# Batch 0 and 1 attention scores with tokens on the partitions, 21 instructions moved to GpSimd, and a rewritten start order

## The chip, the cores and the metric

The kernel runs on one core of a Trainium2 chip. The metric is the device time of one execution in microseconds; the median of several runs counts. A core has five engines that run side by side, each through its own list of instructions in order: TensorE (PE, with its weight loads shown apart as PEld), VectorE (DVE), ScalarE (ACT), GpSimd (POOL) and SyncE (SP), which here issues the loads and stores.

## The reference

The kernel computes an attention over 32 memory slots per head, and feeds the result to a two-layer network. There are 8 batches, 8 heads, 576 tokens, head size 64; the network goes from 512 to 2048 channels and back.

```python
a = softmax(phi, over the 32 slots)                 # phi: b h s m
k_m = einsum("bhsm,bhsd->bhmd", a, k)               # slots of K
v_m = einsum("bhsm,bhsd->bhmd", a, v)               # slots of V
attn = softmax(q @ k_m.T / 8, over the 32 slots)    # b h s m
x = (attn @ v_m) with heads as channels             # 4608 x 512
h = x @ w_in
out = where(h > 0, h, exp(min(h, 0)) - 1) @ w_out
```

## The kernel before

All matrix products are kept at full precision by splitting each operand into a high part and a remainder (HI, LO) and adding three products (PASSES). V's slots are multiplied into w_in ahead of time (`vw`), so that per batch the network's first layer is one product of `vw` with the attention weights `A`.

The work is cut into iterations `it`. One iteration is a batch, a half of its tokens (288, `HALF`) and one block of 128 of the 2048 channels: `hidden` (six PE products into a PSUM bank), `elu_exp` (two ACT instructions), `elu_max` (DVE), `rest_copy` (POOL, the last 32 tokens of the half), `elu_high` (ACT) and `elu_low` (DVE, the remainder), and `project` (six PE products). Iterations 0 to 2 are batch 0's first half, 3 to 5 its second, 6 and 7 its fourth block in both halves; iteration 8 is the first of batch 1.

Before batch 0's first `hidden` stands its attention: `load_phi`, `phi_max`, `phi_exp`, `e_transpose` and `e_copy` turn phi's exponentials; `slots` multiplies them with K or V; `slots_copy`, `slots_transpose` and `kv_copy` put the slots into the tile `kvm`. `scores` multiplies `kvm` with a unit of queries, slots on the partitions. `turn` (DVE, 32x32 block transposes, two instructions per unit) puts tokens on the partitions; `softmax_max`, `softmax_shift`, `softmax_exp`, `softmax_sum` and `softmax_divide` do the softmax; `turn_back` (DVE) transposes back; `probs_high` (ACT) and `probs_low` (DVE) write the two parts of `A`. Batch 0 has three units (160, 128 and 288 tokens), batch 1 two of 288, later batches three of 192.

The weights arrive as 64-bit numbers in 32 tiles k of 128x512 (`load_raw`); even and odd groups of them are w_in (into `win`) and w_out (into `wout`). Each goes through `dec_mag` and `dec_low` (ACT), `dec_sign`, `dec_top` and `dec_add` (DVE; `dec_add` is an addition of 32-bit integers, L410), and for w_out also `dec_high` (ACT) and `dec_rest` (DVE, L424).

Each engine takes its instructions in the order in which the steps are written. For the start, until iteration 64, this order is a list written out by hand, FIRST; an entry such as `vw.0.0.128.256` is a step's name and its arguments. After it a plan sorts the steps by due times; it is the same in both kernels. Loads go through SP's queue in the order of FIRST. Tiles come out of pools with a fixed number of buffers, and an instruction waits for a free one: `gf` has 5, the hidden products' PSUM tile `psh` 2, the raw weight tiles 4 per tag. `warm_up.n` multiplies the identity with itself n times; its result is not used.

## Time and profile before

| | before |
|---|---|
| median of 3 runs (lowest, highest) | 720.07 us (719.92, 722.39) |
| the profiled execution: time, span | 720.75 us, 719.0 us |
| PE busy | 698.5 us (97%) |
| DVE busy | 463.2 us (64%) |
| ACT busy | 459.5 us (64%) |
| POOL busy | 43.4 us (6%) |
| mean granted TensorE clock | 0.985 |
| DMA | 64.45 MB, mean 90 GB/s |

The span runs from the first to the last instruction. An engine's share of the span is an average over stages with different limits, so the stages are read one by one, from windows. Two more things help with the rows below. A matmul of 32-bit floats (f32) is two instructions in the profile, a transpose is one, and a matmul in the format fp32r is one. And a row "x6" merges six instructions that follow each other, with the time that the six took together; in brackets stands how long the engine sat idle before it, and what ended that. In a shape such as "64*32 64x288" the stationary block is 64x32 and the moving one 64x288.

### The profile page before, as it was taken

How to read it: one execution, taken by the hardware profiler on the slowest of the kernel's cores; microseconds unless marked ns; L12 is line 12 of the kernel's file. 1: busy time of each engine (PE TensorE's matmuls, PEld its weight loads, DVE VectorE, ACT ScalarE, POOL GpSimd, SP SyncE). 2: the span in 40 equal slices, each digit the busy share in tenths (PEclk: the TensorE clock that was granted, in tenths of full speed). 3: DMA queues.
4: the chain of work that ended last, by engine and by line, in shares of the span. 5: the costliest groups of instructions: out<-in, count | busy, mean ns of one | idle time of the engine just before them, and what ended most of it. 6: DMA issues, size and time to landing. Idle time of an engine off the chain costs nothing.

```text
span 719.0 us, 13493 instructions
## 1 busy us (share of the span) xinstructions
PE 698.5 (97%) x5050; PEld 575.7 (80%) x5050; DVE 463.2 (64%) x1221; ACT 459.5 (64%) x1102; POOL 43.4 (6%) x88
## 2 busy tenths in 40 slices
PE   7788999999999999999999999999999999999997
...
GB/s 291 361 258 85 171 31 117 122 133 59 137 30 81 205 31 1 96 144 92 1 1 110 145 91 1 13 97 193 31 1 37 90 189 30 2 30 1 30 1 44
DMA packets 24977, 64.45 MB, mean 90 GB/s; under 512 B 3408, under 2 KB 7632, under 8 KB 24912
## 3 DMA queue, kind: packets, MB, share of 16 engines
...
q10 hardware_dynamic: 96, 0.13, 0.1%
HBM read 54.13 MB, written 9.44 MB: 88 GB/s over the span
## 4 chain that ended last, share of the span: by engine, by line
PE 88%; DVE 6%; DMA 3%; ACT 2%; issue 0%; SPq 0%; DVEq 0%; ACTq 0%
PE pso L749 54%; PE psh L688 27%; PE psb L530 3%; DMA kvt<-kv 3%; PE psb L481 2%; PE pso L530 2%; DVE gf L712 1%; DVE top L403 1%; ACT gf L704 0%; DVE wout L424 0%; DVE top L410 0%; ACT gf L703 0%; DVE win L403 0%; DVE win L410 0%; DVE gp L741 0%
## 5 line engine op out<-in xcount | busy, mean ns | idle before, releaser
L749 PE MATMUL pso<-wout,gp 128*128 128x512 f32 x1728 | 444.8, 396 | 0.8 <-ACT orest L812 0.5
L749 PEld LDWEIGHTS pso<-wout,gp 128*128 128x128 f32 x1728 | 310.2, 188 | 66.8 <-issue 2.9
L688 PEld LDWEIGHTS psh<-A,vw 128*128 128x128 f32 x1536 | 229.4, 189 | 40.1 <-issue 10.5
L688 PE MATMUL psh<-A,vw 128*128 128x288 f32 x1536 | 247.7, 298 | 6.7 <-DVE vw L650 3.1
L715 DVE SCALAR_TENSOR_TENSOR gf<-gf,psh 128x256 f32<-128x256 f32 x192 | 80.7, 420 | 144.8 <-ACT gf L704 144.7
L703 ACT ACTIVATE gf<-psh 128x288 f32<-128x288 f32 x256 | 104.7, 409 | 103.2 <-PE psh L688 101.5
L735 ACT CAST gp<-gf 128x256 fp32r<-128x256 f32 x256 | 103.1, 404 | 80.7 <-DVE gf L715 65.7
L741 DVE TENSOR_TENSOR gp<-gf,gp 128x256 fp32r<-128x256 f32 x256 | 108.8, 427 | 52.5 <-ACT gp L735 51.6
L704 ACT ACTIVATE gf<-gf 128x288 f32<-128x288 f32 x256 | 113.9, 445 | 8.1
L291 POOL TENSOR_TENSOR e<-e,nmb 128x512 f32<-128x512 f32 (+1 forms) x18 | 20.7, 1178 | 364.0 <-DMA nmb<-nmd 275.7
L712 DVE SCALAR_TENSOR_TENSOR gf<-gf,psh 128x288 f32<-128x288 f32 x64 | 28.6, 449 | 12.3 <-ACT gf L704 11.5
L723 DVE SCALAR_TENSOR_TENSOR rest<-gf,psh 128x32 f32<-128x32 f32 x192 | 34.6, 180 | 0.0
L731 POOL COPY rest<-gf 128x32 f32<-128x32 f32 x64 | 22.1, 360 | 171.6 <-DVE gf L712 171.5
L650 DVE TENSOR_TENSOR vw<-psb,vw 128x512 fp32r<-128x512 f32 (+2 forms) x48 | 26.9, 582 | 2.0 <-ACT vw L644 2.0
L793 ACT CAST gp<-rest 128x256 fp32r<-128x256 f32 x32 | 12.5, 404 | 22.0 <-PE pso L749 22.0
L798 DVE TENSOR_TENSOR gp<-rest,gp 128x256 fp32r<-128x256 f32 x32 | 13.1, 421 | 16.1 <-ACT gp L793 16.1
L644 ACT CAST vw<-psb 128x512 fp32r<-128x512 f32 (+2 forms) x48 | 22.4, 496 | 0.4 <-PE psb L530 0.4
L530 PE MATMUL psb<-win,kvm 64*32 64x512 f32 (+2 forms) x384 | 22.6, 527 | 0.0
L381 ACT ACTIVATE mag<-raw 128x512 uint32<-128x512 uint32 x30 | 19.9, 673 | 3.3 <-DVE win L403 1.6
L377 ACT ACTIVATE mag<-raw 128x512 f32<-128x512 f32 x30 | 19.6, 665 | 0.0
L650 DVE TENSOR_TENSOR vw<-pso,vw 128x512 fp32r<-128x512 f32 (+1 forms) x28 | 17.2, 624 | 0.0
L481 PE MATMUL psb<-kvt,e 128*32 128x128 f32 (+1 forms) x480 | 15.1, 274 | 0.0
...
## 6 DMA issues: line engine op xcount, KB each, us to landing
...
```

The lines of the kernel that those rows point to most:

```text
L481: nc.tensor.matmul(ps[32 * j : 32 * j + 32, a], s["e"][c // 2][:r, c % 2, x : x + M], kv_rows(b, c, i, 2 * j + a), start=(c == 0 and a == ...
L530: nc.tensor.matmul(outs[a][32 * j : 32 * j + 32, :], lhs[r, 32 * j : 32 * j + 32], rhs[r, j], start=True, stop=True, tile_position=(64 * a ...
L650: nc.vector.tensor_tensor(t[:, LO, a, n0:n1], s["ps"]["vw", c, n0][a], t[:, HI, a, n0:n1], ALU.subtract)
L688: nc.tensor.matmul(ps, t[:, x, g, c0 : c0 + P], s["A"][hf][:, y, g, :], start=(n == 0), stop=(n == 5),)
L703: nc.scalar.activation(gf, ps, AF.Relu, scale=-1.0)
L704: nc.scalar.activation(gf, gf, AF.Exp, scale=-1.0)
L712: nc.vector.scalar_tensor_tensor(gf, gf, -1.0, ps, ALU.add, ALU.max)
L715: nc.vector.scalar_tensor_tensor(gf[:, :n], gf[:, :n], -1.0, ps[:, :n], ALU.add, ALU.max)
L723: nc.vector.scalar_tensor_tensor(rest_of(b, j)[:, o : o + REST], gf[:, n:], -1.0, ps[:, n:], ALU.add, ALU.max)
L735: nc.scalar.copy(gp[:, HI], gs[it][:, : NT * P])
L741: eng.tensor_tensor(gp[:, LO], gf[:, : NT * P], gp[:, HI], ALU.subtract)
L749: nc.tensor.matmul(ps, gp[:, y], wout[j][:, x, :], start=(first and n == 0), stop=(last and n == 2),)
```

## The change

Seven things change at once.

1. In batches 0 and 1 a unit is now half of the tokens (288), and `scores` uses `by_token`: the queries are the stationary block (64 channels x 128 tokens) and the 32 slots the moving one, so the result has tokens on the partitions. The last 32 tokens of a half are done with the slots as before, but also with tokens on the partitions.
2. `turn` is gone there. `softmax_max` and `softmax_shift` read the scores from PSUM, each in two instructions of 288 columns.
3. `back`, new, transposes the weights on PE (four transposes a unit); `turn_back` only transposes the last 32 tokens (two small DVE instructions); `probs_high` and `probs_low` work in two pieces, one of them from PSUM.
4. 18 of the 32 `dec_add` and 3 of the 16 `dec_rest` go from DVE to POOL. `slots_copy` of batch 1 goes from DVE to ACT.
5. There are 38 warm-up products instead of 27.
6. The loads are in another order on SP's queue.
7. FIRST is rewritten up to iteration 64. `hidden` keeps its order except for 5 and 2, 13 and 12, 42 and 40, 60 and 59.

The order up to iteration 8, before and after:

```diff
-tables load_phi.0 phi_max.0.0 load_kv0.K0 load_kv0.K1 load_kv0.T load_raw.0 phi_exp.0.0 phi_max.0.1
-phi_exp.0.1 load_half_q.0.0 warm_up.11 slot_scale.0 load_raw.2 load_kv0.V0 e_transpose.0.1
-e_copy.0.1 e_transpose.0.0 e_copy.0.0 slots.0.0.K.y slots.0.1.K e_transpose.0.2 slots.0.2.K
-slots.0.3.K e_copy.0.2 slots.0.4.K slots_copy.0.K slots_transpose.0.K dec_mag.0 load_raw.1
-load_kv0.V1 dec_sign.0 dec_top.0 kv_copy.0.K dec_low.0 load_raw.3 load_kv.1.1 scores.0.0.yz
-scores.0.1 turn.0.0 turn.0.1 softmax_max.0.0 warm_up.2 warm_up.1 warm_up.2 load_half_q.0.1
-load_phi.1 softmax_max.0.1 softmax_shift.0.0 softmax_shift.0.1 softmax_exp.0.0 dec_add.0
-softmax_exp.0.1 warm_up.1 slots.0.0.V.y slots.0.1.V slots.0.2.V slots.0.3.V slots.0.4.V
-softmax_sum.0.0 slots_copy.0.V slots_transpose.0.V softmax_sum.0.1 load_raw.5 softmax_divide.0.0
-dec_mag.1 softmax_divide.0.1 turn_back.0.0 kv_copy.0.V turn_back.0.1 probs_high.0.0 dec_mag.2
-dec_sign.1 dec_top.1 probs_high.0.1 probs_low.0.0 vw.0.0.0.128.yz vw_high.0.0.0.128 dec_low.1
-dec_sign.2 dec_top.2 vw_low.0.0.0.128 probs_low.0.1 dec_low.2 dec_add.1 hidden.0 dec_mag.3 dec_add.2
-dec_sign.3 dec_top.3 dec_high.1 load_kv.1.0 load_raw.6 load_kv.1.2 elu_exp.0 dec_mag.5 dec_rest.1
-dec_low.3 phi_max.1 scores.0.2.yz vw.0.0.128.256 warm_up.3 vw_high.0.0.128.256 load_kv.1.3
-phi_exp.1.0 load_kv.1.4 phi_exp.1.1 elu_max.0 turn.0.2 vw_low.0.0.128.256 hidden.1 e_transpose.1.1
-e_transpose.1.0 warm_up.3 warm_up.4 softmax_max.0.2 softmax_shift.0.2 elu_exp.1 load_raw.4 dec_add.3
-softmax_exp.0.2 elu_max.1 slot_scale.1 load_raw.12 load_raw.7 load_half_q.1.0 rest_copy.0
-e_transpose.1.2.y elu_high.1 dec_high.3 elu_high.0 e_copy.1.0 softmax_sum.0.2 softmax_divide.0.2
-turn_back.0.2 slots.1.0 slots.1.1 dec_mag.4 dec_sign.4 dec_top.4 dec_sign.5 dec_top.5 probs_high.0.2
-e_copy.1.1 slots.1.2 e_copy.1.2 slots.1.3 dec_mag.7 dec_low.5 slots.1.4 probs_low.0.2 dec_low.4
-dec_mag.6 elu_low.0 dec_add.5 hidden.3 project.0 dec_add.4 dec_high.5 elu_exp.3 slots_copy.1
-dec_rest.3 elu_low.1 elu_max.3 dec_rest.5 vw.0.0.256.384.yz dec_sign.6 dec_top.6 project.1
-vw_high.0.0.256.384 rest_copy.3 rest_copy.1 elu_high.3 slots_transpose.1 vw_low.0.0.256.384
-kv_copy.1 dec_low.6 hidden.4 dec_sign.7 dec_top.7 hidden.2 elu_exp.4 dec_add.6 dec_low.7 scores.1.0
-elu_max.4 elu_exp.2 rest_copy.4 hidden.5 elu_high.4 turn.1.0 elu_max.2 elu_low.3 vw.0.0.384.512
-elu_exp.5 softmax_max.1.0 vw_high.0.0.384.512 rest_copy.2 elu_high.2 vw_low.0.0.384.512
-load_half_q.1.1 scores.1.1.yz hidden.6 elu_max.5 elu_low.2 project.2 vw.1.0.0.256 elu_exp.6
-elu_low.4 softmax_shift.1.0 softmax_exp.1.0 load_raw.9 elu_high.5 hidden.7 dec_mag.12
-vw_high.1.0.0.256 elu_exp.7 turn.1.1 softmax_sum.1.0 elu_max.6 dec_add.7 softmax_divide.1.0
-softmax_max.1.1 project.3 project.4 elu_high.6 load_raw.8 dec_high.7 vw_low.1.0.0.256 elu_max.7
-elu_high.7 dec_mag.9 vw.1.0.256.512 vw_high.1.0.256.512 dec_rest.7 turn_back.1.0 elu_low.5
-softmax_shift.1.1 probs_high.1.0 softmax_exp.1.1 probs_low.1.0 hidden.8 hidden.10 load_raw.17
...
+tables load_phi.0 phi_max.0.0 phi_exp.0.0 phi_max.0.1 phi_exp.0.1 slot_scale.0 warm_up.13
+load_kv0.K0 load_kv0.K1 load_kv0.V1 load_kv0.T load_half_q.0.0 load_raw.0 load_kv0.V0
+e_transpose.0.1 e_copy.0.1 e_transpose.0.0 e_copy.0.0 e_transpose.0.2 e_copy.0.2 warm_up.5
+slots.0.0.K.y slots.0.1.K slots.0.2.K slots.0.3.K slots.0.4.K slots_copy.0.K warm_up.2
+slots_transpose.0.K kv_copy.0.K dec_mag.0 dec_sign.0 dec_top.0 dec_low.0 load_raw.1 load_raw.2
+scores.0.0.yz softmax_max.0.0 warm_up.1 softmax_shift.0.0 warm_up.5 load_half_q.0.1 load_raw.3
+dec_add.0 softmax_exp.0.0 warm_up.2 slots.0.0.V.y slots.0.1.V slots.0.2.V slots.0.3.V slots.0.4.V
+warm_up.1 softmax_sum.0.0 load_raw.6 load_phi.1 load_raw.5 dec_mag.1 dec_mag.2 dec_sign.2 dec_sign.1
+softmax_divide.0.0 dec_top.1 warm_up.1 slots_copy.0.V slots_transpose.0.V kv_copy.0.V
+vw.0.0.0.128.yz vw_high.0.0.0.128 back.0.0.x turn_back.0.0 probs_high.0.0 dec_low.1 dec_top.2
+vw_low.0.0.0.128 dec_sign.3 probs_low.0.0 dec_low.2 phi_max.1 dec_add.1 dec_add.2 dec_mag.3
+warm_up.4 hidden.0 elu_exp.0 dec_mag.5 dec_top.3 dec_sign.5 dec_high.1 dec_low.3 scores.0.1.yz
+vw.0.0.128.256 warm_up.3 vw_high.0.0.128.256 phi_exp.1.0 load_raw.4 load_kv.1.3 load_kv.1.4
+load_kv.1.1 phi_exp.1.1 softmax_max.0.1 vw_low.0.0.128.256 softmax_shift.0.1 dec_rest.1 elu_max.0
+hidden.1 e_transpose.1.0 e_transpose.1.1 softmax_exp.0.1 elu_high.0 load_kv.1.0 load_kv.1.2
+softmax_sum.0.1 dec_top.5 load_raw.9 load_half_q.1.1 load_raw.7 load_raw.11 load_half_q.1.0
+e_copy.1.0 elu_exp.1 dec_mag.4 e_copy.1.1 elu_max.1 elu_low.0 dec_sign.4 softmax_divide.0.1
+dec_add.3 dec_high.3 dec_top.4 slot_scale.1 e_transpose.1.2.y warm_up.1 e_copy.1.2 elu_high.1
+dec_mag.6 dec_low.4 slots.1.0 slots.1.1 slots.1.2 slots.1.3 slots.1.4 back.0.1.b turn_back.0.1
+elu_low.1 dec_rest.3 probs_high.0.1 dec_low.5 dec_mag.7 project.0 probs_low.0.1 hidden.3 dec_add.4
+dec_add.5 vw.0.0.256.384.yz dec_sign.6 slots_copy.1 dec_sign.7 elu_exp.3 dec_top.6 project.1
+rest_copy.1 dec_high.5 slots_transpose.1 dec_low.6 vw_high.0.0.256.384 vw_low.0.0.256.384 kv_copy.1
+hidden.4 dec_rest.5 elu_max.3 dec_top.7 scores.1.0 hidden.5 hidden.2 elu_exp.4 dec_low.7 elu_max.4
+dec_add.6 elu_high.3 rest_copy.4 rest_copy.0 softmax_max.1.0 softmax_shift.1.0 elu_exp.2 elu_max.2
+elu_low.3 vw.0.0.384.512 softmax_exp.1.0 vw_high.0.0.384.512 elu_high.4 rest_copy.3 rest_copy.2
+elu_high.2 elu_exp.5 vw_low.0.0.384.512 load_raw.15 load_raw.8 scores.1.1.yz vw.1.0.0.256 hidden.6
+elu_low.2 softmax_max.1.1 elu_low.4 elu_max.5 project.2 elu_exp.6 softmax_shift.1.1 load_raw.17
+load_raw.10 hidden.7 elu_high.5 elu_max.6 project.3 project.4 load_raw.24 load_raw.12 dec_mag.12
+elu_exp.7 vw_high.1.0.0.256 dec_mag.9 elu_high.6 softmax_sum.1.0 dec_add.7 dec_high.7
+softmax_divide.1.0 back.1.0.h turn_back.1.0 elu_low.5 elu_max.7 elu_high.7 probs_high.1.0
+vw.1.0.256.512 vw_low.1.0.0.256 probs_low.1.0 hidden.8 softmax_exp.1.1 hidden.10 load_raw.13
...
```

The code:

```diff
-             "sc0": 2048, "pr0": 2368, "sc1": 2688, "pr1": 2944, "sc2": 3200, "pr2": 0}
-
-    SPARE1 = {"e0": 0, "e1": 512, "e2": 1024, "x0": 1536,
-              "sc0": 2048, "pr0": 2624, "sc1": 3200, "pr1": 0}
+             "sc0": 2048, "sc1": 2624, "pr0": 3200, "pr1": 3264}
...
     def temp(b, name, i, n):
...
-            o = SPARE1[f"{name}{i}"]
+            o = SPARE[f"{name}{i}"]
...
-    mult_on_pool = ()
-    x_on_act = (0,)
+    mult_on_pool = ((0, 2),)
+    x_on_act = (0, 1)
...
-    rest_on_pool = ()
+    rest_on_pool = (1, 5, 28)
...
-    add_on_pool = ()
+    add_on_pool = (0, 2, 3, 6, 8, 9, 11, 12, 14, 17, 19, 21, 22, 24, 26, 28, 30, 31)
...
     def units(b):
...
-        if b == 0:
-            return (0, 160), (160, 288), (288, 576)
-        if b == 1:
-            return (0, 288), (288, 576)
+        if b < NB:
+            return (0, HALF), (HALF, S)
...
     def bank(shape, where):
...
+    def by_token(outs, q, keys):
+
+        for c in range(NT):
+            for j in range(NPAIR):
+                for a in range(2):
+                    r = slice(64 * a, 64 * a + 64)
+                    n = c * P + j * M
+                    nc.tensor.matmul(
+                        outs[a][:, n : n + M],
+                        q[r, j, c * P : (c + 1) * P],
+                        keys[r, 32 * j : 32 * j + 32],
+                        start=True,
+                        stop=True,
+                        tile_position=(64 * a, 0),
+                    )
+        for a in range(2):
+            for j in range(NPAIR):
+                r = slice(64 * a, 64 * a + 64)
+                nc.tensor.matmul(
+                    outs[a][32 * j : 32 * j + 32, NT * P :],
+                    q[r, j, NT * P :],
+                    keys[r, 32 * j : 32 * j + 32],
+                    start=True,
+                    stop=True,
+                    tile_position=(64 * a, 32 * j),
+                )
+
     def scores(b, u, where="bb"):
...
         ps = [bank([P, q.shape[-1]], x) for x in where]
-        by_head(ps, s["kvm"][:, 0], q)
+        if b < NB:
+            by_token(ps, q, s["kvm"][:, 0])
+        else:
+            by_head(ps, s["kvm"][:, 0], q)
...
     def scores_of(b, own, lent):
...
     def softmax_max(b, u):
+        mx = work.tile([P, 2 * HALF // SQ], F32, name="mx")
+        if b < NB:
+            n = HALF // SQ
+            for a, ps in enumerate(st[b]["ps"]["s", u]):
+                nc.vector.tensor_reduce(
+                    mx[:, a * n : (a + 1) * n],
+                    ps.rearrange("p (n m) -> p n m", m=SQ), AX.X, ALU.max,
+                )
+        else:
+            sc = st[b]["sc"][u]
+            mx = mx[:, : sc.shape[1]]
+            nc.vector.tensor_reduce(mx, sc, AX.X, ALU.max)
+        st[b]["mx", u] = mx
+
+    def softmax_shift(b, u):
+        mx = st[b].pop(("mx", u))
+        if b < NB:
+            n = HALF // SQ
+            sc = temp(b, "sc", u, 2 * HALF).rearrange("p (n m) -> p n m", m=SQ)
+            st[b]["sc"][u] = sc
+            for a, ps in enumerate(st[b]["ps"].pop(("s", u))):
+                g = slice(a * n, (a + 1) * n)
+                nc.vector.tensor_tensor(
+                    sc[:, g], ps.rearrange("p (n m) -> p n m", m=SQ),
+                    mx[:, g].unsqueeze(2).to_broadcast([P, n, SQ]), ALU.subtract,
+                )
+            return
         sc = st[b]["sc"][u]
...
-        mx = work.tile([P, 2 * HALF // SQ], F32, name="mx")[:, :n]
-        nc.vector.tensor_reduce(mx, sc, AX.X, ALU.max)
-        st[b]["mx", u] = mx
-
-    def softmax_shift(b, u):
-        sc = st[b]["sc"][u]
-        n = sc.shape[1]
-        mx = st[b].pop(("mx", u))
         eng = nc.gpsimd if (b, u) in shift_on_pool else nc.vector
...
         eng = nc.gpsimd if (b, u) in mult_on_pool else nc.vector
...
+    def back(b, u, where="b"):
+
+        s = st[b]
+        sc = s["sc"][u].rearrange("p n m -> p (n m)")
+        ps = bank([P, 2, NT * P], where)
+        for a in range(2):
+            for c in range(NT):
+                n = a * HALF + c * P
+                nc.tensor.transpose(ps[:, a, c * P : (c + 1) * P], sc[:, n : n + P], ident)
+        s["ps"]["p", u] = ps
+
     def turn_back(b, u):
...
+        if b < NB:
+            pr = temp(b, "pr", u, 2 * REST)
+            for a in range(2):
+                nc.vector.transpose(
+                    pr[:, a * REST : (a + 1) * REST],
+                    sc[:, (a + 1) * HALF // SQ - 1],
+                )
+            s["pr", u] = pr.rearrange("p (g s) -> p g s", g=2)
+            return
...
     def probs_high(b, u):
...
+        if b < NB:
+            A = s["A"][u] = work.tile([P, 2, 2, HALF], F32R, name="A", bufs=4)
+            nc.scalar.copy(A[:, HI, :, : NT * P], s["ps"]["p", u])
+            nc.scalar.copy(A[:, HI, :, NT * P :], s["pr", u])
+            return
         for hf, src, dst in probs_parts(b, u):
...
     def probs_low(b, u):
...
+        if b < NB:
+            A = s["A"][u]
+            n = NT * P
+            for dst, x in ((slice(0, n), s["ps"].pop(("p", u))), (slice(n, HALF), pr)):
+                nc.vector.tensor_tensor(A[:, LO, :, dst], x, A[:, HI, :, dst], ALU.subtract)
+            return
         eng = nc.gpsimd if (b, u) in low_on_pool else nc.vector
         for hf, src, dst in probs_parts(b, u):
...
-            softmax_divide, turn_back, probs_high, probs_low, vw, vw_high, vw_low, hidden,
+            softmax_divide, back, turn_back, probs_high, probs_low, vw, vw_high, vw_low, hidden,
...
```

173 lines of the change are left out of this document (86 added, 87 removed).

## The prediction

> **What bounds the kernel now.** First the page's table of engines and its 40 slices: PE holds 97% of the span, so time can only come out of the few slices where PE is not at 9.
>
> ```profile
> PE 698.5 (97%) x5050; PEld 575.7 (80%) x5050; DVE 463.2 (64%) x1221; ACT 459.5 (64%) x1102; POOL 43.4 (6%) x88
> ...
> PE   7788999999999999999999999999999999999997
> ```
>
> Then the windows between three landmarks read off PE's timeline: the first hidden product of batch 0 (25.91 us), the first of its second half (hidden.3, 40.38) and the first of batch 1 (hidden.8, 60.60).
>
> ```profile
> 0.00:25.91 25.91, 17.57 (x254) 14.24 (x254) 12.20 (x33) 10.46 (x26) 0.70 (x6) 0.71 0.94 327
> 25.91:40.38 14.47, 11.52 (x155) 9.01 (x155) 14.01 (x30) 11.93 (x26) 0.21 (x1) 0.82 1.03 351
> 40.38:60.60 20.22, 16.97 (x171) 12.02 (x167) 19.70 (x45) 15.51 (x40) 1.65 (x4) 1.00 0.57 210
> 60.60:200.00 139.40, 138.89 (x940) 113.60 (x940) 115.13 (x245) 111.27 (x260) 23.32 (x62) 1.00 0.30 100
> ```
>
> The columns are the busy time of PE, PEld, DVE, ACT and POOL, then granted clock, DMA share and GB/s. After 60.60 PE is busy 138.89 of 139.40 us: what DVE loses there cannot show. Before, three regimes follow each other: DMA (share 0.94), then DMA and DVE together (1.03, and 14.01 of 14.47), then DVE alone (19.70 of 20.22, DMA 0.57). The chain of waits agrees: a load until 20.6 us, then DVE up to hidden.8; its last rows here give PE's prices, 0.80 for a hidden and 1.39 for a project step.
>
> ```profile
> 8.47 12.04 DMA kvt<-kv
> ...
> 59.85 0.70 DVE A L630
> 60.60 1.61 PE psh L688 x10
> ...
> 76.18 0.80 PE psh L688 x6
> 76.98 1.39 PE pso L749 x6
> ```
>
> So the change is worth the shift of hidden.8 in time, less the PE work that it leaves behind that point.
>
> **The change, part by part.** *DVE's relief, 25.91 to 60.60.* Prices, from DVE's timeline (start, duration):
>
> ```profile
> 34.70 0.73 DVE L588 TENSOR_REDUCE sm<-spare 128x18 f32<-128x576 f32 x1
> 35.46 0.18 DVE L589 TENSOR_SCALAR sm<-sm 128x18 f32<-128x18 f32 x1
> ...
> 35.98 0.76 DVE L599 TENSOR_TENSOR spare<-spare,rs 128x576 f32<-128x576 f32 x1
> 36.77 0.78 DVE L605 STREAM_TRANSPOSE spare<-spare 128x576 f32<-128x576 f32 x1
> ...
> 38.58 0.42 DVE L398 TENSOR_SCALAR top<-raw 128x512 uint32<-128x512 uint32 x1
> ...
> 39.64 0.75 DVE L630 TENSOR_TENSOR A<-spare,A 128x576 fp32r<-128x576 f32 x1
> 40.31 0.42 DVE L741 TENSOR_TENSOR gp<-gf,gp 128x256 fp32r<-128x256 f32 x1
> 40.65 0.68 DVE L410 CUSTOM_DVE_ANT_0 top<-top,mag 128x1024 uint16<-128x1024 uint16 x1
> ...
> 42.19 0.68 DVE L424 TENSOR_TENSOR wout<-top,wout 128x512 fp32r<-128x512 f32 x1
> ...
> 47.62 0.84 DVE L563 STREAM_TRANSPOSE win<-psb 128x288 f32<-128x288 f32 x2
> ```
>
> Back to back each starts some 0.08 before the one ahead has ended: an addition (L410) or a weight remainder (L424) takes 0.60, a unit's two score turns 0.76, a turn back 0.70. Gone are three units' turns (2.3), three turns back (2.1), additions 2, 3 and 6 (1.8), remainders 1 and 5 (1.2) and slots_copy.1, now on ACT (0.3): 7.7. In come two 32-column transposes a unit (by the 0.18 row, 1.0), maxima and shifts in two halves (+0.09 each, from 0.42 at 256 columns and 0.75 at 576: 0.5), probs_low in two pieces (0.4): 1.9. Net 5.8 of 33.7, which leaves 27.9.
>
> *PE's burden.* The prices, from PE's timeline; the second row ran at half clock, the others at full.
>
> ```profile
> 8.59 0.65 PE L481 MATMUL pso<-kvt,spare 128*32 128x64 f32 x32 [0.77 <-DMA kvt<-kv]
> ...
> 15.89 2.93 PE L828 MATMUL pso<-ident 128*128 128x128 f32 x12
> ...
> 32.91 1.03 PE L459 MATMUL psb<-ident,ph 128*128 128x128 f32 x8
> 33.79 1.73 PE L828 MATMUL pso<-ident 128*128 128x128 f32 x14
> ...
> 46.59 0.71 PE L530 MATMUL psb<-one,kvm 64*32 64x288 f32 x16
> ...
> 48.75 0.45 PE L530 MATMUL psb<-win,kvm 64*32 64x128 f32 x16
> ...
> 57.19 0.73 PE L530 MATMUL psb<-win,kvm 64*32 64x256 f32 x16
> ```
>
> A back step is four transposes at 0.13: 0.5 a unit, 2.0 in all. A unit of scores was 16 instructions in 0.7; by_token makes 48 (each f32 product is two), 32 of them with 64x128 stationary and only 32 moving columns. No row shows that shape. Below it lie the slot products, 20 ns each: 48 make S = 1.0 us a unit. Above it lie the warm-up products, 124 ns with as many stationary columns and four times the moving ones: 32 x 0.124 + 16 x 0.02 = 4.3. A gain on 0.7 is excluded by the count. I take S = 2.0, near the geometric middle, because the two heads alternate between halves of the array and the 0.71 row shows tiles overlapping. For the weight load the Trainium skill, "TensorE: Matmul & The Clock Gate", section "LDWEIGHTS (loading the stationary operand)", divides the columns by 1.2 to get ns; by that rule, with loads one behind the other, a unit would cost 32 x 0.107 + 0.3 = 3.7, an estimate, and the time would be 721 to 724. No run here shows such a load by itself.
>
> *To the first hidden product.* SP's queue changes: V1 goes ahead of T, raw0 behind the queries, raw2 behind V0. With eight loads in flight SP issues a load when the eighth before it has landed, so its starts are landings:
>
> ```profile
> 8.47 0.33 SPq L312 DMA_DIRECT2D kvt<-kv  x1
> ...
> 12.18 0.33 SPq L302 DMA_DIRECT2D kvt<-kv  x1
> ...
> 14.70 0.33 SPq L262 DMA_DIRECT2D ph<-phiT  x1
> ...
> 20.58 2.87 SPq L302 DMA_DIRECT2D kvt<-kv  x3
> ...
> 28.34 2.08 SPq L341 DMA_DIRECT2D one<-q  x2
> 32.31 1.92 SPq L369 DMA_DIRECT2D raw<-w_in  x2
> ```
>
> These are K0, T, the queries, V1, kv.1.0 and kv.1.2. T moves back by one 512 KB load, 1.3 us; V1 comes some 7 us earlier, so V stops being the gate and the softmax is next. Its ACT prices, exp and probs_high:
>
> ```profile
> 33.91 0.67 ACT L582 ACTIVATE spare<-spare 128x576 f32<-128x576 f32 x1
> ...
> 37.58 0.67 ACT L622 CAST A<-spare 128x576 fp32r<-128x576 f32 x1 [0.74 <-DVE spare L605]
> ```
>
> Scores start at 15.7, one us later than now (T gates them, not the queries), and last 4.0 at half clock. Behind them: maxima 0.84, shifts 0.84, exp 0.67, sum with reciprocal 1.2, two dec_signs 0.75, divide 0.77, back 0.7, probs_high 0.8, probs_low 0.75, hand-overs 0.5: 7.8. hidden.0 at 27.5, 1.6 later than now. The eleven extra warm-up products (38 against 27) sit in PE's waits; without that cover their 22 instructions cost 2.7 us at full and 5.4 at half clock. What they may buy is the clock, 0.71 on average before hidden.0; I book nothing.
>
> *hidden.0 to hidden.3.* DVE's new list, by the prices above and their sizes: phi_max 1.3, three dec_top 2.1, two dec_sign 0.7, dec_add.1 and dec_rest.3 1.2, softmax 4.0, probs_low 0.75, vw_low 0.4, elu steps 1.4, slot_scale 0.3, in all 12.1, and 0.5 of waiting for exp: 40.1. PE's new order has all of batch 1's slot products ahead of back.0.1, and kv.1.2 now closes 10.75 MB of the queue instead of 9.44; at 351 GB/s it lands 3.7 us later, at 36.0. Then slots 1.6, back 0.6, probs_high 0.9, probs_low 0.9: 40.0. Both meet; hidden.3 stays near 40.1, with project.0 already done, which it was not before.
>
> *hidden.3 to hidden.8.* DVE needs 15.4 (19.70 now): signs and tops of two tiles 2.1, three additions 1.8, vw_low 1.5, elu steps 3.6, softmax of one unit 4.0 and of the next as far as its shift 1.7, probs_low 0.75. PE needs six hidden at 0.80, four projects at 1.39, vw 2.2, slot transposes 0.4, back 0.5 and 2S = 4.0: 17.5. PE decides: 57.6, 3.0 before 60.60. Behind it stays back.1.1, 0.5. Sum: -3.0 + 0.5 = -2.5. The profiled execution took 720.75 (its span 719.0 and 1.75 around it), so 718.25; against the median of the runs, 720.07, it is 717.6.
>
> *POOL.* Its nearest rows are two groups of shifts of e, two inputs of the additions' size; then two DVE remainders that ran inside the second group.
>
> ```profile
> 179.19 2.58 POOL L291 TENSOR_TENSOR e<-e,nmb 128x512 f32<-128x512 f32 x2 [1.96 <-DMA e<-phi]
> ...
> 239.50 3.46 POOL L291 TENSOR_TENSOR e<-e,nmb 128x512 f32<-128x512 f32 x3 [39.38 <-DMA nmb<-nmd]
> ```
>
> ```profile
> 240.64 0.45 DVE L741 TENSOR_TENSOR gp<-gf,gp 128x256 fp32r<-128x256 f32 x1 [0.38 <-ACT gp L735]
> ...
> 242.83 0.43 DVE L741 TENSOR_TENSOR gp<-gf,gp 128x256 fp32r<-128x256 f32 x1 [0.38 <-ACT gp L735]
> ```
>
> So 1.3 us each, 27 us for 21. Queued behind them are the rest_copys, which hold the gf buffers that ACT's elu_exp needs, and on ACT dec_high.3 waits for dec_add.3. PE's two open hidden products cover one such 1.3; without that cover it costs 1.3 each time. The 14 additions behind 60.60 and remainder 28 gain nothing. The remainders' 0.45 and 0.43 stand against 0.42 elsewhere: no mutual block. The Trainium skill, "SBUF — State Buffer", section "Who interferes with whom", says that a DVE instruction with two SBUF inputs and a GpSimd one that reads SBUF exclude each other for the whole instruction. The trace does not agree with that in these two rows; what the rule would do is the third rival.
>
> *The rest.* Batch 2's softmax keeps its instructions; the moved order around hidden.64 gets no price, at most 1 us either way. mult_on_pool names a unit that no longer exists.
>
> **The rivals.** (1) *The relief comes through.* The stationary blocks load behind running products, S = 1.0: PE 15.5, DVE 15.4 beside it, hidden.8 at 55.6: -5.0 + 0.5, 715.6; if the clock rises early too, some 2 less. For it: DVE's 97%. Against: the DMA share of 1.03 ahead of hidden.3.
> (2) *Stationary loads serialize; slower.* S = 4.3, at half clock 8.3. Scores end at 20 to 24, hidden.0 at 27.8 to 31.8, hidden.3 at 40.4 to 44.4, PE 22.1 behind it: hidden.8 at 62.5 to 66.5, with back.1.1 +2.4 to +6.4, 722.5 to 726.5. From S = 3.2 on the gain is gone. For it: 124 ns a warm-up product; against: overlapping tiles.
> (3) *POOL blocks DVE.* Three long POOL instructions ahead of hidden.3 add 3.9 to DVE's 40.1: +3.9 on the sum, 721.5.
>
> **How the numbers follow.** Measuring tells about 0.5%, 3.6 us, from no change. Forecast 0.46, its own range 715.8 to 720.0; rival 1 0.31, 713.5 to 716.4; rival 2 0.14; rival 3 0.09, 720 to 724. Faster takes rival 1 and the forecast's low end: 0.35. Slower takes most of rival 2 and a little of rival 3: 0.13. The rest is within 0.5%: 0.52. The range 713.8 to 723.4 leaves out rival 1's lowest end and most of rival 2.
>
> **What would show it.** In the profile after: 48 instructions a unit on by_token's lines, some 2 us a unit; the last slot products of batch 1 held by a kvt load and ended near 37.6; hidden.0 near 27.5, hidden.3 near 40, hidden.8 near 57.6; 28 us of DVE between the first and the last. A unit over 3.2 us, remainders beside POOL stretched well beyond 0.6, or slot products held by nothing would make it wrong. If hidden.8 comes early and the span does not follow, my reading of PE behind 60.60 is wrong.

## The result: 0.8% slower

The changed kernel takes 726.34 us (median of 6 runs, 725.14 to 728.57), the kernel before 720.2 beside it (6 runs). The ratio is 1.0082 with a 95% interval of 1.0059 to 1.0105. The forecast was 717.6 in a range of 713.8 to 723.4: the wrong side, and outside. The profiled execution took 725.14, its span 723.3, which is 4.3 more than the 719.0 of before.

From the page of the kernel after, the engines and PE's slices:

```profile
PE 704.9 (97%) x5200; PEld 583.6 (81%) x5200; DVE 453.3 (63%) x1197; ACT 459.3 (64%) x1106; POOL 68.0 (9%) x109
...
PE   7999999999899999999999999999999999999997
```

DVE lost 10 us of work (463.2 before) and the start is denser (PE's second to fourth slices read 7, 8, 8 before and read 9 now). But there is now an 8 behind the start, in the eleventh slice (181 to 199 us). The windows of the kernel after, at the same landmarks as in the prediction (hidden.0, hidden.3 and hidden.8 are now at 26.71, 39.99 and 60.61), then the stretch behind them in two pieces:

```profile
0.00:26.71 26.71, 20.95 (x308) 18.67 (x309) 10.05 (x25) 10.11 (x24) 1.98 (x7) 0.87 0.93 330
26.71:39.99 13.28, 11.75 (x185) 9.61 (x185) 12.10 (x29) 12.71 (x29) 4.22 (x4) 1.00 1.03 345
39.99:60.61 20.62, 18.91 (x230) 15.10 (x228) 16.16 (x42) 14.96 (x40) 3.38 (x6) 1.00 0.64 240
60.61:180.00 119.39, 117.84 (x722) 96.00 (x723) 97.66 (x205) 100.02 (x235) 36.04 (x64) 1.00 0.25 76
180.00:200.00 20.00, 17.93 (x207) 14.70 (x206) 9.86 (x22) 9.78 (x25) 4.47 (x10) 1.00 0.63 203
```

The same two last pieces in the kernel before:

```profile
60.60:180.00 119.40, 118.89 (x728) 97.44 (x729) 103.62 (x220) 100.49 (x233) 19.14 (x52) 1.00 0.30 96
180.00:200.00 20.00, 20.00 (x214) 16.16 (x212) 11.52 (x26) 10.78 (x27) 4.18 (x11) 1.00 0.33 122
```

Two things went wrong. hidden.8 did not come early. And behind it, where PE had been idle for 0.51 us in 139.4, it is now idle for 1.55 + 2.07 = 3.62.

**The lag as a second measure.** The six products of each `hidden` can be found in both traces, so the start of every step can be compared. The lag of a step is its first product's start in one kernel minus that of the step in the same place in the kernel before (minus means earlier). hidden.8's own first product starts at 59.80 before and 59.89 after; the 60.60 and 60.61 of the windows are its third, which waits for `probs_low`. The lags of all kernels below, in microseconds, with the ratio of all their runs to those of the kernel before (each group of runs had its own, with medians from 720.2 to 721.47):

| kernel | hidden.8 | hidden.20 | hidden.36 | hidden.57 | hidden.64 | ratio, 95% interval |
|---|---|---|---|---|---|---|
| after | +0.1 | +0.5 | +1.7 | +1.8 | +4.2 | 1.0082, 1.0059 to 1.0105 |
| x1_load12 | -2.4 | -2.2 | -1.0 | -1.0 | +1.3 | 1.0035, 1.0022 to 1.0047 |
| y4_tail55 | -2.5 | -2.3 | -1.1 | -1.0 | -0.7 | 1.0018, 1.0007 to 1.0029 |
| z1_mid | -2.3 | -2.0 | -2.5 | -2.4 | -2.0 | 0.9973, 0.9961 to 0.9984 |
| x2_tail | -1.1 | +1.1 | +0.7 | +2.0 | +1.9 | 1.0065, 1.0053 to 1.0077 |
| y2_tail12 | -0.8 | +1.2 | +0.9 | +2.2 | +2.1 | 1.0028, 1.0018 to 1.0038 |
| y3_tail12_late_dve | -2.9 | -2.7 | -3.0 | -3.0 | -3.0 | 0.9980, 0.9969 to 0.9992 |
| y1_late_dve | -1.4 | +0.4 | +2.7 | +3.4 | +6.0 | 1.0093, 1.0077 to 1.0108 |
| x3_nopool | +1.6 | +3.5 | +5.9 | +6.5 | +10.8 | 1.0137, 1.0121 to 1.0153 |
| x4_before_pool | -0.2 | +2.6 | +2.2 | +3.5 | +3.4 | 1.0046, 1.0034 to 1.0058 |
| z2_y3_nopool | +0.3 | +0.4 | +0.1 | +0.1 | +0.7 | 1.0004, 0.9993 to 1.0015 |
| z3_warm27 | -1.0 | -0.8 | -1.1 | -1.2 | -0.7 | 0.9989, 0.9973 to 1.0004 |

A lag is that of one execution, and executions of a kernel differ by some 3 us and more: in one group of runs of the kernel before, 719.43 us went with a mean granted clock of 0.992 and 724.11 with 0.983. The clock is below 1 in the start alone (0.77 and 0.72 in the first two stretches of 20 us of the kernel before, 0.91 and 1.00 in y4). So a single lag at hidden.8 is good to a microsecond or two (x2's profiled execution was the fastest of its six, 722.85 against a median of 725.70; the six kernels with the start of the change and load_raw.12 moved up have hidden.8 at -0.8 to -2.9), and the ratios count for the verdicts. A step of the lag within one row is much better: the granted clock is 1.00 there.

### The profile page after: what moved, and what is told of

It reads as the page before. It is cut to its first block, busy times and chain, and to the rows that moved or that the text cites. A ratio compares the mean times of both kernels' runs of the same rounds, so it can differ in the third digit from the quotient of the medians.

```text
span 723.3 us, 13798 instructions
## 1 busy us (share of the span) xinstructions
PE 704.9 (97%) x5200; PEld 583.6 (81%) x5200; DVE 453.3 (63%) x1197; ACT 459.3 (64%) x1106; POOL 68.0 (9%) x109
## 4 chain that ended last, share of the span: by engine, by line
PE 84%; DMA 7%; ACT 4%; DVE 3%; SPq 1%; issue 1%; POOL 0%; ACTq 0%; POOLq 0%; DVEq 0%
PE pso L822 51%; PE psh L761 26%; PE psb L523 3%; DMA raw<-w_out 2%; PE psb L474 2%; PE pso L523 2%; DMA kvt<-kv 2%; DMA raw<-w_in 2%; DMA e<-phi 1%; ACT gf L777 1%; ACT gf L776 1%; DVE gf L785 1%; ACT gp L808 1%; DVE gp L814 1%; DMA nmd<-nm 0%
## 5 line engine op out<-in xcount | busy, mean ns | idle before, releaser
L776 ACT ACTIVATE gf<-psh 128x288 f32<-128x288 f32 x256 | 105.1, 410 | 99.5 <-PE psh L761 97.4
L814 DVE TENSOR_TENSOR gp<-gf,gp 128x256 fp32r<-128x256 f32 x256 | 114.4, 449 | 50.6 <-ACT gp L808 49.9
L785 DVE SCALAR_TENSOR_TENSOR gf<-gf,psh 128x288 f32<-128x288 f32 x64 | 28.7, 449 | 22.5 <-ACT gf L777 17.8
L804 POOL COPY rest<-gf 128x32 f32<-128x32 f32 x64 | 19.2, 324 | 91.9 <-DVE gf L785 91.8
L403 POOL TENSOR_TENSOR win<-win,mag 128x512 uint32<-128x512 uint32 x10 | 13.2, 1328 | 41.1 <-ACT mag L374 37.3
```

The source lines that it names most:

```text
L776: nc.scalar.activation(gf, ps, AF.Relu, scale=-1.0)
L785: nc.vector.scalar_tensor_tensor(gf, gf, -1.0, ps, ALU.add, ALU.max)
L814: eng.tensor_tensor(gp[:, LO], gf[:, : NT * P], gp[:, HI], ALU.subtract)
```

## The experiments

Three losses show in the row of the kernel after: no gain at hidden.8, then +1.2 between hidden.20 and hidden.36 (at 90 to 128 us), then +2.4 between hidden.57 and hidden.64 (at 179 to 215 us). Two theories were put against each other: O, the new order of steps and loads makes them; P, the instructions moved to GpSimd make them by blocking DVE.

### First group: one load, the tail of the order, GpSimd on and off

**x1_load12.** In the kernel after, the chain of work that ended last goes through a load ahead of hidden.8 (start, duration, what):

```profile
47.66 0.38 SPq L362
48.04 0.05 issue
48.09 7.45 DMA raw<-w_out
55.54 0.02 issue
55.56 0.02 ACT mag L370
...
60.61 1.47 PE psh L761 x9
```

This is tile 12. The kernel before issued it by 27.4 us, right behind load_raw.4; the change put it behind load_raw.24.

```diff
-load_half_q.1.0 e_copy.1.0 ... load_raw.17 load_raw.10 hidden.7 ... load_raw.24 load_raw.12 dec_mag.12
+load_half_q.1.0 load_raw.12 e_copy.1.0 ... load_raw.17 load_raw.10 hidden.7 ... load_raw.24 dec_mag.12
```

> The changed kernel with one load moved: load_raw.12 stands right behind load_half_q.1.0 instead of behind load_raw.24. Theory O (the new order makes the loss): ACT's dec_mag.12 waited 1.7 us for that load at 55.5 us and held elu_exp.7, the vw casts and with them hidden.8 behind it; with the load early hidden.8 should start 1.5 to 2.5 us before 60.6, and the time fall by about as much, to some 724. Theory P (the 21 instructions on POOL block DVE): nothing in front of hidden.8 but two stretched DVE instructions, so hidden.8 stays within 0.5 us and the time within 0.5 us.

Measured: 723.92 us, 1.0035. ACT's timeline in the kernel after, where `dec_mag.12` waits, and behind it `elu_exp.7` (L776):

```profile
55.56 0.67 ACT L370 ACTIVATE mag<-raw 128x512 f32<-128x512 f32 x1 [1.72 <-DMA raw<-w_out]
56.13 0.39 ACT L776 ACTIVATE gf<-psh 128x288 f32<-128x288 f32 x1
```

The same two instructions in x1, then PE's hidden.8 and the window from hidden.3 to hidden.8 there:

```profile
52.79 0.66 ACT L370 ACTIVATE mag<-raw 128x512 f32<-128x512 f32 x1
53.36 0.40 ACT L776 ACTIVATE gf<-psh 128x288 f32<-128x288 f32 x1
```

```profile
57.37 2.20 PE L761 MATMUL psh<-A,vw 128*128 128x288 f32 x12
```

```profile
39.05:57.36 18.31, 18.28 (x227) 14.81 (x225) 15.42 (x40) 14.36 (x39) 3.38 (x6) 1.00 0.76 280
```

The wait is gone and hidden.8 starts at 57.37; between the two landmarks PE is busy for 18.28 of 18.31 us. One load in the wrong place of the queue had taken most of the gain of the start. How much is better read from the ratios than from this one lag, of which 0.9 us was there already at hidden.3 (39.05 against 39.99), ahead of the wait: the load moved up is worth 3.4 us here (1.0082 to 1.0035) and 2.7 us in the pair x2 and y2 below (1.0065 to 1.0028). Behind hidden.8 the two other losses stay, +1.2 and +2.3.

**x2_tail.** The kernel after up to hidden.11, then the order of the kernel before; the additions stay on GpSimd.

```diff
 FIRST = (order after, up to hidden.11)
-        + (order after, hidden.11 to hidden.64)
+        + (order before, hidden.11 to hidden.64)
```

> The changed kernel up to hidden.11, and from there the order of the kernel before (its loads of weights included where they are still to be issued); POOL keeps its 21 instructions. Theory O: the two steps in the lag, 1.4 us at 102 to 110 us and 2.4 us at 183 to 186 us, go; hidden.64 starts within 1 us of 215 instead of 219, and the time is 3 to 4 us below the changed kernel's. Theory P: the stretched DVE instructions stay, so at least 2 us of the loss behind hidden.11 stay as well.

Measured: 725.70 us, 1.0065. The step at 179 to 215 us is gone, but the lag now rises by 1.9 between 76 and 86 us and by 1.2 between 137 and 163 us, places at which the kernel after loses next to nothing. Of the loss behind hidden.11, 2.7 us stay, as theory P expected, and the time is not the 3 to 4 us lower that theory O expected. So the old order does not fit the new assignment either.

**x3_nopool.** The kernel after with nothing moved to GpSimd.

```diff
-    rest_on_pool = (1, 5, 28)
-    add_on_pool = (0, 2, 3, 6, 8, 9, 11, 12, 14, 17, 19, 21, 22, 24, 26, 28, 30, 31)
+    rest_on_pool = ()
+    add_on_pool = ()
```

> The changed kernel with all additions and remainders back on DVE, the order unchanged. Theory P: nine DVE instructions that ran 0.3 to 1.0 us too long beside a long POOL instruction (7.0 us in all) run at their usual length, and the time falls by 3 us or more. Theory O: DVE gets 21 x 0.60 = 12.6 us of work back and loses 7.0 us of stretch; the time stays within 1.5 us of the changed kernel's or gets longer.

Measured: 731.39 us (4 runs), 1.0137. By the two ratios GpSimd saves 4 us with the new order; it is not what makes the net loss. Theory P falls as the explanation of the result, though not for the old order, as the next run shows.

**x4_before_pool.** The reverse: the kernel before with those 21 instructions on GpSimd, and nothing else.

```diff
-    rest_on_pool = ()
-    add_on_pool = ()
+    rest_on_pool = (1, 5, 28)
+    add_on_pool = (0, 2, 3, 6, 8, 9, 11, 12, 14, 17, 19, 21, 22, 24, 26, 28, 30, 31)
```

> The kernel before with the 18 additions and 3 remainders on POOL and nothing else changed. Theory P: slower than before by 2 us or more. Theory O: within 1 us of before, or faster by up to 3 us, since DVE sets the pace up to hidden.8 and is rid of five of these instructions there.

Measured: 724.41 us, 1.0046, as theory P expected. hidden.8 moves by 0.2 us only, and 3.6 us are lost behind it. With the old order the move costs time; with the new one it saves time.

### Second group: order and GpSimd apart, behind hidden.8

All four have load_raw.12 as in x1.

**y1_late_dve.** x1 with the additions from tile 8 on and remainder 28 on DVE.

```diff
-    rest_on_pool = (1, 5, 28)
-    add_on_pool = (0, 2, 3, 6, 8, 9, 11, 12, 14, 17, 19, 21, 22, 24, 26, 28, 30, 31)
+    rest_on_pool = (1, 5)
+    add_on_pool = (0, 2, 3, 6)
```

> The changed kernel with load_raw.12 moved up (as in x1), and the 14 additions from tile 8 on and the weight remainder 28 back on DVE; only additions 0, 2, 3, 6 and remainders 1, 5 stay on GpSimd. x1 gained 2.4 us at hidden.8 and lost 1.3 of it at 102 to 112 us and 2.3 at 182 to 187 us. Theory P (the late GpSimd instructions block DVE and make the loss at 102 to 112): that loss goes, hidden.64 comes 1.3 earlier than in x1, ratio to the kernel before 1.001 to 1.002. Theory O (the new order makes both losses; DVE now has 14 more instructions in an order made without them): 1.0035 as x1, or up to 2 us more.

Measured: 727.41 us, 1.0093: against theory P, and more of a loss than theory O allowed. **y2_tail12** is x2 with load_raw.12 moved up:

> The changed kernel up to hidden.11 with load_raw.12 moved up, and behind hidden.11 the order of the kernel before; the additions stay on GpSimd. Theory O: with the old order behind it the 2.4 us of hidden.8 stay, ratio 0.997. Theory P: the old order has no room for the GpSimd additions (x4, the kernel before with them, lost 2.6 by 88 us and 3.4 in all), so the 2.4 us are used up by 88 us: ratio 1.000 to 1.003.

Measured: 722.61 us, 1.0028, as theory P expected. **y3_tail12_late_dve** has both edits, the old order behind hidden.11 and y1's two lines:

> As the kernel before it in this list, but with the additions from tile 8 on and remainder 28 on DVE: start of the changed kernel, rest of the kernel before. Both theories (the start is worth 2.4 us and nothing behind it takes them back): hidden.8 at 57.4 to 58, lag constant at -2.4 to -2.0 from there to hidden.64, ratio 0.9965 to 0.998, faster than both kernels. If the gain at hidden.8 only lets PE run into a later wait (my forecast's reading that PE behind 60.60 is full would be wrong in general): lag back to 0 by 110 us, ratio 1.000.

Measured: 719.22 us (12 runs), 0.9980. Behind hidden.8 the four ratios are: new order with GpSimd 1.0035 (x1), new order with DVE 1.0093, old order with GpSimd 1.0028, old order with DVE 0.9980. Each order runs best with the assignment that it came with: P is right for the old order, where the late instructions on GpSimd cost 3.5 us, and wrong for the new one, where they save about 4. In y3 the gain of the start, 2.9 us at hidden.8, stays to the microsecond up to hidden.64: when nothing else is wrong behind hidden.8, an early hidden.8 is worth what it is early.

**y4_tail55.** x1 with the old order from hidden.55 on, and batch 2's `load_kv` at hidden.51 again.

```diff
-load_kv.2.1 dec_high.29 ... hidden.55 (order after: load_kv.2.2 to 2.4 behind hidden.56, hidden.60 ahead of slots.2)
+load_kv.2.1 load_kv.2.2 load_kv.2.3 load_kv.2.4 dec_high.29 ... hidden.55 (order before)
```

> x1 with the order of the kernel before from hidden.55 on (slots of batch 2 and project.56 ahead of the next hidden, batch 2's kv loads issued at hidden.51 and not beside the loads of e). Theory O: the step of 2.3 us at 182 to 187 us goes, lag -1.0 stays to hidden.64, ratio about 1.0005. If the step is made by the later load of nm and e alone and not by the order around it: it stays, 1.0035.

Measured: 722.12 us, 1.0018, a little above the ratio expected. Of the 2.3 us behind hidden.57, 0.4 are left. What they were, in the kernel after, on PE, ACT and POOL:

```profile
185.87 1.07 PE L761 MATMUL psh<-A,vw 128*128 128x288 f32 x6 [2.07 <-DVE gf L785]
```

```profile
183.85 0.63 ACT L289 ACTIVATE e<-e 128x512 f32<-128x512 f32 x1 [2.23 <-POOL e L284]
184.39 0.39 ACT L776 ACTIVATE gf<-psh 128x288 f32<-128x288 f32 x1
```

```profile
182.52 2.54 POOL L284 TENSOR_TENSOR e<-e,nmb 128x512 f32<-128x512 f32 x2 [2.96 <-DMA e<-phi]
```

Read from the bottom: the load of e is late (issued at 175.22, 172.92 before, of which 1.8 us are the lag that the kernel has there), GpSimd's shift waits for it, ACT's `e_exp` waits for the shift, and in ACT's queue `elu_exp` (L776) stands behind `e_exp`; so DVE's `elu_max` and PE's next `hidden`, whose PSUM buffer it frees, are late. The kernel before has the same wait on ACT, 1.92 us, but PE had a project step and the 80 slot products to do meanwhile:

```profile
180.52 0.63 ACT L296 ACTIVATE e<-e 128x512 f32<-128x512 f32 x1 [1.92 <-POOL e L291]
```

```profile
181.83 1.71 PE L749 MATMUL pso<-wout,gp 128*128 128x512 f32 x6
183.47 2.52 PE L481 MATMUL psb<-kvt,e 128*32 128x128 f32 x80
```

In y4 ACT's wait is still there, 2.13 us, and PE, which again has a project step and the slot products behind hidden.58, does not wait:

```profile
179.84 0.63 ACT L289 ACTIVATE e<-e 128x512 f32<-128x512 f32 x1 [2.13 <-POOL e L284]
```

The wait is not new; its cover is gone.

### Third group: the middle, GpSimd in the start, the warm-up

**z1_mid.** y4 with the old order also from hidden.21 to hidden.32.

```diff
-hidden.21 ... project.21 hidden.25 ... hidden.26 hidden.28 ... project.22 hidden.27 ... project.23 ... hidden.32
+hidden.21 ... project.21 ... hidden.25 ... project.22 ... hidden.26 ... project.23 ... hidden.28 hidden.27 ... hidden.32
```

> The kernel y4 (changed kernel, load_raw.12 moved up, old order from hidden.55 on), and the old order also from hidden.21 to hidden.32; the additions stay on GpSimd as the change put them. Theory O (order alone makes the loss of 1.3 us at 102 to 112 us): the three PE waits there go, the lag of -2.4 us at hidden.8 lasts to hidden.64, ratio 0.9993 to 1.0003 by the 0.0014 a microsecond of the other runs. Theory P (the GpSimd additions make it whatever the order): lag -1.0 or worse behind 112 us, ratio 1.0018 or more.

Measured: 719.55 us, 0.9973: better than the ratio expected. The step at 90 to 128 us is gone; PE is busy for 119.31 of 120.00 us from 60 to 180 us. The kernel after has hidden.25, 26 and 28 in a row there, with project.22 behind them. With two PSUM buffers, 26 and 28 each wait for the `elu_max` (L785) of the step two places ahead; a third wait, of a project step for `elu_low` (L814), follows. Together they come to 0.88 us of the 1.2:

```profile
102.32 1.06 PE L761 MATMUL psh<-A,vw 128*128 128x288 f32 x6 [0.22 <-DVE gf L785]
103.69 1.07 PE L761 MATMUL psh<-A,vw 128*128 128x288 f32 x6 [0.31 <-DVE gf L785]
...
110.28 1.44 PE L822 MATMUL pso<-wout,gp 128*128 128x512 f32 x5 [0.35 <-DVE gp L814]
```

Together, x1, y4 and z1 take back 2.9 + 2.0 + 1.4 us of lag at hidden.64 (from +4.2 to -2.0), with all 18 additions on GpSimd. By the ratios the three are worth 3.4, 1.2 and 3.2 us, so the split is known to a microsecond or two only. The sum is the whole loss, and it lay in the order of steps and loads.

**z2_y3_nopool.** y3 without the last four additions and two remainders on GpSimd (both lists empty).

> The kernel y3 (start of the change, rest of the kernel before) with the last four additions (0, 2, 3, 6) and two remainders (1, 5) back on DVE too: nothing is on GpSimd that was not before. If the relief by GpSimd is part of the start's gain: DVE has six instructions of 0.6 us more ahead of hidden.8, which comes 1.5 to 3.5 us later than in y3, ratio to the kernel before 1.000 to 1.003. If the start's gain is all from the scores' new orientation (in the kernel before, x4, the same six instructions on GpSimd moved hidden.8 by 0.2 us alone): within 0.5 us of y3, ratio 0.998.

Measured: 722.12 us, 1.0004. hidden.8 comes at +0.3 instead of -2.9. The new start gains nothing by itself, the move to GpSimd in the old order neither (x4, -0.2 at hidden.8); together they gain 1.7 us by the ratios and 3.1 by the lags.

**z3_warm27.** y3 with 27 warm-up products.

```diff
-warm_up.13 ... warm_up.5 ... warm_up.5 ... warm_up.4
+warm_up.11 ... warm_up.2 ... warm_up.2 ... warm_up.1
```

> The kernel y3 with 27 warm-up products instead of 38 (13 to 11, 5 to 2 twice, 4 to 1). My forecast booked nothing for them. If that holds: within 1 us of y3. If they lift the clock: the granted clock ahead of hidden.8 falls (y3 has 0.85 and 0.98 in the first two stretches of 20 us) and the time rises by 1 to 4 us.

Measured: 720.53 us, 0.9989. In its profiled execution the granted clock was 0.80 and 0.77 in the first two stretches of 20 us, against 0.85 and 0.98 in y3. It is so over all 12 runs of each: the mean granted clock was 0.991 to 0.995 in y3 and 0.983 to 0.993, at the middle 0.988, in z3, as in the kernel before (0.983 to 0.992). So the eleven products, which the prediction booked at nothing, do go with a higher clock. The times of both kernels spread over 3 to 6 us and the intervals overlap, so whether they pay stays open.

**z4_shift_dense** belongs to the question of how GpSimd blocks DVE, below.

```diff
-        d = dram.tile([P, 2], F32, name="nmd")
-        nc.sync.dma_start(d, s["nm"])
-        s["nmb"] = work.tile([P, P, 2], F32, name="nmb", bufs=1)
+        d = dram.tile([2, P], F32, name="nmd")
+        nc.sync.dma_start(d.rearrange("a x -> x a"), s["nm"])
+        s["nmb"] = work.tile([P, 2, P], F32, name="nmb", bufs=1)
```

> The kernel before, with the two maxima that GpSimd's shifts of e add (nmb) laid out in two runs of 128 numbers and not in pairs, so that the shift's second input has no stride. In the kernel before, DVE remainders inside these shifts keep their 0.42 to 0.45 us, while beside the additions on GpSimd they take up to 1.5. If the stride of the second input decides whether the two engines shut each other out: remainders inside the shifts now take 0.9 to 1.5 us. If something else does (the integers, for one): they stay at 0.42 to 0.55.

Measured: 750.67 us, one run, and no answer: in all six batches DVE's remainder came only 0.23 to 0.24 us before the end of a shift, and took 0.51 to 0.52 us. Writing the maxima in single numbers took the 1 KB store 7.8 us (the list of DMA issues: size, median from issue to landing) instead of 2.9, and ACT held `elu_high` (L735) and `elu_exp` behind `e_exp`, as it held `elu_exp` in the kernel after, only longer:

```profile
nmd<-nm SPq DMA_DIRECT2D x6, 1.0 KB, 7.8
```

```profile
253.99 0.63 ACT L296 ACTIVATE e<-e 128x512 f32<-128x512 f32 x1 [4.15 <-POOL e L291]
```

```profile
254.95 0.52 DVE L741 TENSOR_TENSOR gp<-gf,gp 128x256 fp32r<-128x256 f32 x1 [4.56 <-ACT gp L735]
```

PE's waits for `elu_high` come to 14.6 us in six places; where the rest of the 30 us went stays open. The question itself is answered by the trace of before, below.

### Fourth group: does the stride decide whether GpSimd blocks DVE?

GpSimd's additions stretch DVE instructions. In y2, POOL's and DVE's timelines, and PE's next hidden:

```profile
81.29 1.35 POOL L403 TENSOR_TENSOR win<-win,mag 128x512 uint32<-128x512 uint32 x1 [1.63 <-ACT gf L776]
```

```profile
81.52 1.67 DVE L396 SCALAR_TENSOR_TENSOR top<-mag,top 128x512 uint32<-128x512 uint32 x1
83.12 0.80 DVE L785 SCALAR_TENSOR_TENSOR gf<-gf,psh 128x288 f32<-128x288 f32 x2
```

```profile
83.61 0.66 PE L761 MATMUL psh<-A,vw 128*128 128x288 f32 x3 [0.65 <-DVE gf L785]
```

`dec_top` (L396) takes 1.67 instead of 0.69: it starts 0.23 behind the addition and ends 0.55 behind its end, so it did its work afterwards. `elu_max` and PE are late by it; a wait of 0.68 us at 79.17 and this one make up 1.33 of the 1.9 us that y2 loses there. The prediction had read from two remainders inside the shifts of e that nothing of this kind happens. The shifts read their second input with a stride of two numbers, so the three kernels here store ACT's `dec_low` in pairs, and the additions read with that stride.

```diff
+        if k in add_on_pool:
+            nc.scalar.mul(lows[k].rearrange("p (n a) -> p a n", a=2),
+                          raws.pop(k)[:, :, 0].rearrange("p (a n) -> p a n", a=2), 2.0**-29)
...
+            t = t.rearrange("p (a r) n -> p a r n", a=2)
+            low = lows.pop(k).rearrange("p (r n a) -> p a r n", a=2, n=P)
+            nc.gpsimd.tensor_tensor(t, t, low, ALU.add)
```

**w1_x4_stride** (x4 with this):

> The kernel x4 (the kernel before with the 18 additions and 3 remainders on GpSimd), with the 18 remainders of ACT (dec_low) stored in pairs, so that GpSimd's additions read their second input with a stride of two numbers, as its shifts of e do. x4 lost 3.4 us, and 8 DVE instructions beside the additions were stretched by 0.4 to 1.15 us. If the stride of the second input decides: those beside the additions keep their 0.42 to 0.69 us (the three beside the remainders, L424, stay stretched), the loss falls to 0 to 1 us, ratio 1.000 to 1.0015. If the integers or something else decides: stretched as in x4, ratio 1.004 to 1.006 (more, if the strided addition itself takes longer than 1.3 us).

Measured: 724.47 us, 1.0046, as x4. **w2_y2_stride** (y2 with this):

> The kernel y2 (start of the change, old order behind hidden.11, additions on GpSimd) with the same storing in pairs. y2 lost 1.9 us at 76 to 83 us and 1.2 at 140 to 163 us, y3 (late additions on DVE) nothing. If the stride decides whether GpSimd shuts DVE out, and that made y2's loss: lag constant behind hidden.13, ratio 0.998 as y3. If y2's loss is from late results of GpSimd and not from DVE shut out: it stays, 1.0028, though no DVE instruction is stretched. If the stride decides nothing: as y2, 1.0028.

Measured: 723.03 us, 1.0028. **w3_after_stride** (the kernel after with this):

> The changed kernel with the same storing in pairs. Its loss was put down to the order (load_raw.12, 102 to 112 us, 182 to 187 us: together 6.2 us in x1, y4, z1), not to GpSimd: ratio 1.006 to 1.0085 if that holds whatever the stride does, at most 1 us better. If DVE shut out by GpSimd makes the waits at 102 to 112 us after all: 1.3 us better or more, ratio 1.005 to 1.0065, and no PE wait there.

Measured: 727.76 us, 1.0094 (1.0075 to 1.0114), above the ratio expected and no better than the kernel after. The ratios of w1 and w2 are those of x4 and y2, and so are the stretched instructions (in w1 `dec_top` again):

```profile
82.70 1.69 DVE L410 SCALAR_TENSOR_TENSOR top<-mag,top 128x512 uint32<-128x512 uint32 x1
```

The stride has no part in it. What misled the prediction is found in the rows themselves. Its row "239.50 3.46 ... x3" merges three shifts. POOL's timeline of the kernel before from a later start shows where the second begins:

```profile
240.76 2.19 POOL L291 TENSOR_TENSOR e<-e,nmb 128x512 f32<-128x512 f32 x2
```

The remainder at 240.64 had started 0.12 before that, in the hand-over between two shifts, and the one at 242.83 in the last 0.12 of the third. One batch later the same trace has the lock in plain sight, with the strided shifts of e and nothing of the change: here the remainder starts 0.07 behind a shift, and takes 1.53 us.

```profile
318.90 2.20 POOL L291 TENSOR_TENSOR e<-e,nmb 128x512 f32<-128x512 f32 x2
```

```profile
318.97 1.53 DVE L741 TENSOR_TENSOR gp<-gf,gp 128x256 fp32r<-128x256 f32 x1 [0.37 <-ACT gp L735]
```

Another, at 408.92, takes 1.30 us. So what z4 and the prediction took as given, that remainders inside the shifts keep their 0.42 to 0.45 us, was not so, and the question of the stride could have been answered from the trace of before. In x4 the pair of 240.64 meets with GpSimd ahead, and the remainder takes 1.49 us:

```profile
242.66 2.58 POOL L291 TENSOR_TENSOR e<-e,nmb 128x512 f32<-128x512 f32 x2 [39.16 <-DVE gp L741]
```

```profile
244.03 1.49 DVE L741 TENSOR_TENSOR gp<-gf,gp 128x256 fp32r<-128x256 f32 x1 [0.38 <-ACT gp L735]
```

## Why the prediction was wrong, step by step

- *Scores by token, S = 2.0 a unit.* Right. At full clock the 32 instructions with 128 stationary columns took 1.98 us, 62 ns each, and the 16 for the last tokens 0.2 to 0.3; at half clock 3.63 and 0.36:

```profile
14.91 3.63 PE L539 MATMUL pso<-kvm,qh 64*128 64x32 f32 x32 [0.35 <-ACT kvm L515]
18.47 0.36 PE L550 MATMUL pso<-kvm,qh 64*32 64x32 f32 x16
...
28.16 1.98 PE L539 MATMUL pso<-kvm,qh 64*128 64x32 f32 x32
...
36.54 1.65 PE L474 MATMUL psb<-kvt,win 128*32 128x128 f32 x48 [0.20 <-ACT wout L410]
38.12 0.66 PE L651 MATMUL psb<-ident,spare 128*128 128x128 f32 x4
...
39.99 1.11 PE L761 MATMUL psh<-A,vw 128*128 128x288 f32 x6
```

  The loads of the stationary blocks, on PEld, show why:

```profile
28.16 1.86 PEld L539 LDWEIGHTS pso<-kvm,qh 64*128 64x128 f32 x32 [0.17 <-issue]
```

  In the trace they start in pairs, one load for each half of the array, at full clock a pair every 111 ns. The rule of the Trainium skill, "TensorE: Matmul & The Clock Gate", section "LDWEIGHTS (loading the stationary operand)", gives 107 ns for 128 columns, and the trace agrees with that within each half. What did not come is "one behind the other", which the 3.7 us a unit had assumed: the two halves load side by side, and an instruction costs 62 ns. Rival 2 fell with it.
- *hidden.0 and hidden.3.* Near: 26.71 against 27.5, 39.99 against 40.1. For hidden.0 there is luck in it: kernels with the same start have it between 23.97 (y4) and 27.86 (y2), hidden.3 between 38.90 and 40.69. Batch 1's slot products ended near 38.1, against 37.6. Their first 32 were held by a load; the wait ahead of the last 48 is put down to ACT, 0.20 us, not to a load, as the prediction had asked:

```profile
35.26 1.08 PE L474 MATMUL psb<-kvt,win 128*32 128x128 f32 x32 [0.93 <-DMA kvt<-kv]
```

- *DVE's relief.* Right: 12.10 + 16.16 = 28.3 us between the first and the last landmark, against 27.9.
- *hidden.8 at 57.6.* Wrong by 3.0. The step "PE decides: 57.6" had costed the queue for the queries and batch 1's data, but not for the weight tiles: load_raw.12 had been moved back by 20 us in it (from 27 to 48), and ACT's list stood behind it, 1.72 us. With that load put back, hidden.8's first product came at 57.37 and its third, the landmark of the forecast, at 57.97 (x1), and PE's own work up to the first was 18.28 where the forecast had 17.5.
- *"After 60.60 PE is busy 138.89 of 139.40 us: what DVE loses there cannot show."* Wrong, and with the next step the costliest. It is a statement about the old order, read as one about the stage. PE was full there because ACT's and DVE's steps were placed so that each wait had cover. y3, with that order and assignment, keeps the gain; the new order lost 1.2 us at 90 to 128 with additions on GpSimd, 2.4 with them on DVE (y1). The prediction named this failure, but only for an early hidden.8.
- *"The moved order around hidden.64 gets no price, at most 1 us either way."* Mis-sized: 2.4 us, from hidden.60 placed ahead of batch 2's slots; y4 took back 2.0 of it.
- *"POOL: no mutual block."* Wrong; the lock is there. In the kernel after nine DVE instructions beside GpSimd's additions and remainders are stretched by 0.30 to 1.04 us, 7 us together. This is what the Trainium skill, "SBUF — State Buffer", section "Who interferes with whom", states: a DVE instruction with two inputs in SBUF contends with a GpSimd instruction that reads SBUF, and whoever comes first has the shared port for the whole instruction. Here the traces agree with it, also at 318.97 in the kernel before. Still rival 3 did not decide: ahead of hidden.3 only one DVE instruction was stretched, by 0.45, and taking the 21 instructions off GpSimd made the kernel slower (x3).
- *Moving additions behind 60.60 gains nothing.* Wrong in both directions: by the ratios it costs 3.5 us with the old order (y2 against y3) and saves about 4 with the new one (x1 against y1).

None of the rivals was the case that came. A rival "the new order uncovers waits behind hidden.8" was missing; its price could have been read from the waits that had cover in the trace of before, such as ACT's 1.92 at 180.52.

Two versions beat both kernels: z1_mid, 0.9973, and y3_tail12_late_dve, 0.9980. With -0.2 to -0.3% both lie below the 0.5% that the prediction called measurable; their intervals exclude 1.
